# The inverse's first stage as pairs of 64-row tiles, w2 loaded in three pieces, and another total order of the work

## The chip, the cores and the metric

The kernel runs on one core of a Trainium2 chip. A core has five engines that run side by side and meet only at semaphores: PE (matrix multiply, with a separate path that loads weights, called PEld in the profile), ACT and DVE (elementwise work; these two can also read PSUM, the memory into which PE writes), POOL (elementwise work in SBUF) and SP, which here only issues DMAs. The metric is the device time of one launch in microseconds (us); smaller is better. Each kernel is run several times and the median counts. A profile is one execution recorded by the hardware.

## What is computed

Two sublayers follow each other: a gated long convolution over the normalised input, with a residual, and an MLP with the Mish activation over the normalised result, with a residual. 2048 positions (S), 640 channels (D), hidden width 1728, bf16 in and out.

```python
k_shift = sum(k_pad[:, t:t+S, :] * shift_k[:, ks-1-t] for t in range(4))   # 4-tap causal
kv  = k_shift * v
kv_f = rfft2(pad(kv, 2*S));  kf_f = rfft2(pad(ssm_k, 2*S))
y   = irfft2(kv_f * kf_f)[:S].astype(bf16)          # causal convolution, one per channel
A   = layernorm(q) * (y + kv * ssm_D)
h   = q + A
f   = einsum("bsd,df->bsf", layernorm(h), w1) + b1
act = f * tanh(softplus(f))                          # Mish
out = h + einsum("bsf,fd->bsd", act, w2)
```

## The kernel before

The transforms are matmuls with cosine and sine tables. Channels are held in five groups of 128 (dc 0 to 4); in one group four channels and 32 places make the 128 partitions. Positions are split as t = 16 t1 + t2, so that a transform over 4096 points becomes a 128-point one (stage 1), a small one with twiddles for each of 128 frequencies f (stage 2), and their inverses. The stages, with the names that the order below uses:

- **d_...**: loads. n is ssm_k (five pieces), k, v and x (the input q) four pieces each, g the 4 MB table of stage 2 (eight), sk the tiny shift_k, cst a table for stage 1 and masks, dr ssm_D, w1 and w2 the MLP's weights, t2m the table of the inverse's second stage. DMAs of SP go out in SP's order, and each waits until the DMA eight before it (over all queues) has landed. d_cst, d_sk and d_dr are issued by ACT.
- **k1pe, k1ev**: ssm_k transposed on PE, and copied out of PSUM. dadd adds ssm_D to its first point.
- **cfpe, coef, wsh**: shift_k spread over the partitions by one matmul; DVE copies it, POOL makes four banded matrices (wsh0 to 3) of it.
- **ktpe, ktev, ktsh**: k transposed; **kspe, kv**: the 4-tap filter as matmuls with wsh, and the product with v on DVE.
- **s1kpe, s1kev / s1vpe, s1vev**: stage 1 for ssm_k and for kv, 20 groups each. A group is 16 matmuls into one PSUM buffer of 1024 columns and one copy out of it ("eviction").
- **s2kpe, s2kev / s2vpe, s2vev**: stage 2, 22 groups for ssm_k, 20 for kv (8 for channel groups 0 and 1, 4 for group 2, 8 for 3 and 4). It overwrites its own input. All 22 for ssm_k are needed before the **sw** copies: ten DMAs inside SBUF that exchange real and imaginary rows.
- **pr**: 20 products of the two spectra on DVE, four for each channel group.
- **i1pe, i1ev**: the inverse's first stage (I1), 20 groups, four for each channel group; a group's matmuls need all four products of it.
- **i2a/i2b/i2pe, y**: the inverse's second stage, one step for each of the 16 row tiles of 128 positions, needing all I1 evictions; y is its eviction.
- **ln1, ln1p, lnx**: the input's layernorm (statistics on DVE, a power on POOL, the normalised tile by ACT or POOL). **wb, h, bn, pow, hc**: product, residual, statistics, power, normalised result; **tr** transposes it by DMA, the first two tiles on PE (**trpe, trev**).
- **m1pe, hb**: first MLP matmul in five units of 256, 256, 512, 512, 512 positions, Mish on ACT. **m2pe, res, d_out**: second matmul, residual, store. In m2pe the last 64 hidden rows of two row tiles are done as a pair of matmuls on 64 rows each (L671).

There is no scheduler at run time. ORDER (L26) lists 660 operations in one total order by name; the engines execute theirs in this order and wait by semaphores for what others must have done. A token `name@2` puts the result in PSUM buffer 2 (there are four, ps0 to ps3, of 1024 fp32 columns); `:d`, `:a`, `:p` choose DVE, ACT or POOL where there is a choice; evictions without a letter go to ACT, except k1ev and ktev, which go to DVE. `_ordered` (L108) reads it. The evictions run through `ev` (L259): L261 on ACT, L263 on DVE.

I1 multiplies the product tile (as weights, 128 rows of real and imaginary parts) with two tables, a12, 128 by 128 each. Each of these is zero except where the channel index of row and column agree, four channels in all:

```python
for dgl in range(8):
    b, l = dc * 8 + gi * 2 + dgl // 4, dgl % 4
    for k in range(2):
        nc.tensor.matmul(pz[:, dgl, :], KS[:, k, b, :, l], a12[:, k, :], start=k == 0, stop=k == 1)
```

SBUF areas are shared over time: the tile ks holds first the spectra (KS, two halves of 20480 columns), then the MLP's activations, w2 (from column 20480) and the convolution's row tiles tt (from column 30720).

Of the kernel before, what the change touches and what calls it, by code (L numbers as in the profile page):

```python
# [13 lines left out]
BF16 = mybir.dt.bfloat16  # L14
# [12 lines left out]
d_dr wz idn d_n0 cz wm@0 small lane d_n1 d_cst d_sk d_n2 warm d_n3 d_n4 d_g0 dsel dcol dadd0 d_k2 k1pe0@1 d_k3 dadd1:p k1pe1@2 d_a12 k1ev0b d_k0 k1ev0  # L27
s1kpe0_3@3 k1ev1 s1kpe0_1@0 s1kev0_3 d_k1 s1kpe0_0@1 dadd2 s1kev0_1 s1kpe1_3@2 s1kev0_0:d dadd3:p d_g4 s1kpe0_2@3 k1pe2@0 s1kev0_2 dadd4:p d_g1
s1kev1_3 kz b1pe@1 k1pe4@3 k1ev2 c_b1 cfpe@2 k1pe3@1 k1ev4:a coef d_v0 s1kpe2_0@0 k1ev3 wsh1 s1kpe2_1@2 s1kev2_0 s1kpe4_3@3 d_g7 s1kev2_1:d s1kpe3_1@1
s1kev4_3 s1kpe2_2@0 wsh3 s1kpe1_0@2 s1kev3_1 d_v1 s1kev2_2:d s1kpe4_1@3 d_g2 s1kev1_0 s1kpe3_2@1 s1kev4_1:d s1kpe1_2@0 s1kev3_2 d_g6 ktpe0_0@2 wsh2  # L30
ktpe0_3 ktpe0_2 s1kev1_2 ktpe2_0@3 ktpe2_3 ktpe2_2 d_v2 ktpe2_1 ktpe0_1 ktev2 ktpe1_0@1 ktev0:a ktpe1_1 ktpe1_3 ktpe1_2 s1kpe3_3@0 d_g5 ktev1 ktsh2
s1kpe4_0@3 s1kev3_3 s1kpe1_1@2 ktsh0 s1kev4_0:d d_v3 s1kpe4_2@1 wsh0 s1kev1_1 s1kpe3_0@0 s1kev4_2:d s1kpe2_3@3 s1kev3_0 d_g3 ktpe4_0@2 ktpe4_2 ktpe4_3
s1kev2_3 ktsh1 ktpe3_0@1 ktpe4_1 ktpe3_3 ktev4 ktpe3_1 ktpe3_2 s2kpe_6@0 s2kpe_12@3 ktev3 s2kev_6 kspe0_0@2 s2kev_12 s2kpe_18@0 kv0_0 ktsh3 kspe2_0@1
s2kev_18 ktsh4 s2kpe_42@3 kv2_0 kspe3_0@2 s2kev_42 s2kpe_96@0 kv3_0 s2kpe_24@1 s2kev_96 kspe4_0@3 s2kev_24 kspe1_0@2 kv4_0 s2kpe_108@0 kspe1_1@1 kv1_0
s2kev_108 s2kpe_72@3 kspe0_1@0 d_x1 s2kev_72 kv1_1 d_x0 s2kpe_66@2 s2kpe_102@3 s2kev_66 kv0_1 kspe4_1@1 s2kev_102 s2kpe_120@2 kv4_1 kspe3_1@0
s2kev_120 s2kpe_126@3 kv3_1 s2kpe_78@1 s2kev_126 s2kpe_0@2 s2kev_78 s2kpe_114@3 s2kev_0:d s2kpe_36@0 s2kev_114 s2kpe_54@1 s2kev_36:d s2kpe_84@2
s2kev_54 s2kpe_60@3 s2kev_84 ln1_0 kspe2_1@1 s2kev_60 s2kpe_48@0 kv2_1 ln1p0 s1vpe0_2@2 s2kev_48 s1vpe1_1@3 s1vev0_2:d s1vpe2_1@1 d_x2 s1vev1_1
s1vpe1_0@0 d_x3 s1vev2_1 s1vev1_0:d s1vpe4_3@2 s1vpe3_2@3 s1vev4_3 s1vpe0_0@1 s1vev3_2:d s1vpe2_2@0 s1vev0_0 s2kpe_90@2 s1vpe1_2@3 s1vev2_2 s2kev_90:d
# [8 lines left out]
pr4_32 i1pe1_0@0 i1ev2_0 i1pe2_2@3 pr4_64 i1ev1_0 i1pe2_1@2 ln1_8 i1ev3_2 i1pe2_3@0 i1ev2_2 ln1_6 ln1p8 i1pe4_3@1 i1ev2_3 ln1_11 i1pe4_0@3 ln1p6
i1ev2_1 i1ev4_3:d i1pe4_2@0 i1ev4_0 lnx6:p i1pe4_1@2 ln1_4 i1ev4_2 ln1p11 i2a1@1 d_w2a i1ev4_1 ln1_14 i2a0@3 d_w2b ln1p4 d_w2c i2b1 ln1_10 i2a2@0 y1
i2b0 i2pe4@2 y0 wb1 i2pe5@1 y4 h1 i2pe8@3 wb0 y5 h0 i2b2 i2a3@2 y8 bn1 i2pe15@1 y2 i2b3 i2pe12@3 bn0 y15 pow1 i2pe13@0 y3 i2pe11@1 pow0 y12 hc1 wb2
trpe1@2 y11 i2pe7@3 hc0 y13 h2 trpe0@1 trev1:a wb3 i2pe6@0 bn2 trev0:a i2pe10@2 y7 m1pe0_3@1 h3 lnx11 pow2 bn3 m1pe0_2@3 y6 hc2 y10 pow3 ln1_7  # L50
# [16 lines left out]
SW_PIECES = 1  # L67
V_PIECES = 4
# [57 lines left out]
def _make_tables():  # L126
# [3 lines left out]
    g = np.arange(16, dtype=np.float64)  # L130
    T = {}
# [13 lines left out]
    T["g"] = np.moveaxis(G, 4, 6).reshape(128, 128 * 128)  # L145
# [14 lines left out]
    a12 = np.stack([np.moveaxis(A1, 0, 2).reshape(128, 128), np.moveaxis(A2, 0, 2).reshape(128, 128)], axis=1)  # L160
# [3 lines left out]
    T["t2m"] = np.concatenate([t2m.reshape(128, 4096), a12.reshape(128, 256)], axis=1)  # L164
# [5 lines left out]
def kernel(  # L170
# [49 lines left out]
    a12_t = cpool.tile([P, 256], BF16, name="a12_t")  # L220
# [24 lines left out]
    w2 = ks[:, 20480:20480 + 15 * D].rearrange("p (c d) -> p c d", c=15)  # L245
    tt_s = [ks[:, 30720 + t * D:30720 + (t + 1) * D] for t in range(NT)]
# [219 lines left out]
    d_a12 = load("d_a12", a12_t[:], dram["t2m"][:, 4096:4352])  # L466
# [3 lines left out]
    for dc in range(NDC):  # L470
        for gi in range(4):
            p_ = pt()

            def pe(e, gi=gi, p_=p_, dc=dc):
                pz = p_.f32().rearrange("p (g n) -> p g n", g=8)
                for dgl in range(8):
                    b, l = dc * 8 + gi * 2 + dgl // 4, dgl % 4
                    for k in range(2):
                        nc.tensor.matmul(pz[:, dgl, :], KS[:, k, b, :, l], a12[:, k, :], start=k == 0, stop=k == 1)  # L479
# [10 lines left out]
    def emit_w2(e):  # L490
        nc.sync.dma_start(w2[:, 0:13, :], B_w2[0:13 * P, :].rearrange("(c p) d -> p c d", p=P))
    d_w2 = [OP("d_w2a", "sp", i1_pes, emit=emit_w2)]
# [241 lines left out]
```

## Time and profile before

| | |
|---|---|
| median of 3 runs | 225.41 us |
| lowest, highest | 225.4, 225.89 us |
| profiled execution, first to last instruction (span) | 223.5 us |
| PE busy in it | 214.0 us, 96% |
| DVE, ACT busy | 133.2 and 133.0 us, 60% and 59% |
| POOL busy | 58.9 us |
| moved by DMA | 30.98 MB, mean 139 GB/s |

The profile gives the execution's time as its span; what lies around the span (the launch and the last store's end) is in the runs' times, which are 1.9 us longer at the median.

How to read its rows. A row of a timeline is: start, length (both us), engine, line, operation, out<-in by tile name, shapes, count; in brackets the idle time of that engine before it and what ended it. A row of the groups is: line, engine, operation, shape, count | busy us, mean ns of one | idle us before them. A DMA row ends with KB each and us from issue to landing. Matmuls overlap in the pipeline, so the length of one is more than its share; busy time divided by the count is nearer to what one costs. A row of the chain is start, length, engine, tile and line.

### The profile page before, as it was taken

The page shows a single profiled execution, that of the slowest core. Times are in us where ns is not written, and L with a number is a line of the kernel's source. Part 1 is how long each engine was busy: PE and PEld are TensorE (multiplying, and loading weights), DVE is VectorE, ACT ScalarE, POOL GpSimd, SP SyncE. Part 2 cuts the span into 40 slices and gives each one's busy share as a digit, 9 for nine tenths or more (in the row PEclk, how much of TensorE's full clock was granted, in tenths as well). Part 3 has the DMA queues.
Part 4 walks back from the last instruction along what each step waited for, and adds up shares of the span by engine and source line. Part 5 has one row for each costly group of instructions (what it writes and reads, how often), then busy time and mean ns, then how long its engine had stood idle before and what let it go on. Part 6 is the DMA issues. An engine that isn't in the chain of part 4 may idle for free.

```text
span 223.5 us, 6119 instructions
## 1 busy us (share of the span) xinstructions
PE 214.0 (96%) x2645; PEld 157.6 (70%) x2650; DVE 133.2 (60%) x232; ACT 133.0 (59%) x182; POOL 58.9 (26%) x120
## 2 busy tenths in 40 slices
PE   7899999999879999889999999999999999999994
PEld 2899999888869999458877644444567444766763
DVE  2776899999989999889878999100002200022122
ACT  2389888999999999999983015565600075200000
POOL 5147620102860005347887523100000000000000
PEclk9999999999999999999999999999999999999999
DMA  5999994372991789303004443500001100010211
GB/s 181 390 413 409 412 374 121 143 239 93 375 415 69 258 331 290 124 0 62 1 0 62 84 123 91 118 0 0 3 0 59 59 3 0 0 56 6 76 54 49
DMA packets 19563, 30.98 MB, mean 139 GB/s; under 512 B 10704, under 2 KB 14928, under 8 KB 18768
## 3 DMA queue, kind: packets, MB, share of 16 engines
q1 hardware_dynamic: 19104, 30.46, 39.0%
q8 instruction: 21, 0.34, 0.7%
q10 hardware_dynamic: 336, 0.12, 0.2%
q14 instruction: 6, 0.05, 0.1%
q0 software_dynamic: 96, 0.00, 0.0%
HBM read 20.42 MB, written 2.62 MB: 103 GB/s over the span
## 4 chain that ended last, share of the span: by engine, by line
PE 70%; DVE 13%; DMA 9%; ACT 4%; issue 2%; SPq 1%; POOL 1%; DVEq 0%
PE ps L663 26%; PE ps L598 25%; DVE ks L461 6%; DMA ks<-in_B_w_dram 4%; DMA ks<-ks 3%; PE ps L396 3%; PE ps L422 3%; ACT uv L261 3%; DMA ks<-in_A_ssm_k_dram 3%; PE ps L341 2%; PE ps L376 2%; DVE ks L263 2%; PE ps L357 2%; DVE ra L362 1%; PE ps L397 1%
## 5 line engine op out<-in xcount | busy, mean ns | idle before, releaser
L620 ACT ACTIVATE ks<-ps,b1s 128x512 bf16<-128x512 f32 (+1 forms) x69 | 36.1, 610 | 42.8 <-PE ps L598 30.3
L663 PE MATMUL ps<-ks 128*128 128x320 bf16 (+2 forms) x420 | 58.4, 299 | 0.0
L598 PE MATMUL ps<-G 128*128 128x512 bf16 (+1 forms) x320 | 57.0, 336 | 0.3
L688 DVE TENSOR_TENSOR rb<-ps,rb 128x640 bf16<-128x640 f32 x15 | 11.7, 816 | 68.9 <-PE ps L671 66.5
L663 PEld LDWEIGHTS <-ks 128*128 128x128 bf16 x420 | 40.6, 98 | 17.2 <-issue 1.3
L598 PEld LDWEIGHTS <-G 128*128 128x128 bf16 x325 | 31.3, 98 | 24.4 <-issue 1.1
L261 ACT CAST uv<-ps 128x1024 bf16<-128x1024 f32 x49 | 45.2, 1197 | 0.0
L261 ACT CAST ks<-ps 128x960 bf16<-128x960 f32 (+3 forms) x49 | 39.8, 905 | 8.1 <-PE ps L397 5.0
L461 DVE TENSOR_TENSOR ks<-ks,uv 128x2048 bf16<-128x2048 bf16 x20 | 23.1, 1225 | 0.7 <-DMA ks<-ks 0.7
L422 PEld LDWEIGHTS <-G 128*128 128x128 bf16 x512 | 20.9, 96 | 3.1 <-issue 2.5
L479 PE MATMUL ps<-a_t,ks 128*128 128x128 bf16 x320 | 18.8, 219 | 0.4 <-DVE ks L461 0.3
L479 PEld LDWEIGHTS <-ks 128*128 128x128 bf16 x320 | 18.3, 113 | 0.7 <-DVE ks L461 0.6
L422 PE MATMUL ps<-uv,G 128*128 128x64 bf16 (+1 forms) x384 | 12.8, 186 | 1.8 <-ACT uv L261 1.8
L544 DVE BATCH_NORM_STATS2 st<-rb 128x6 f32<-128x320 bf16 x32 | 14.0, 478 | 0.1
L515 POOL TENSOR_SCALAR ve<-mv 128x1 f32<-128x1 f32 x16 | 4.7, 292 | 34.9 <-DVE mv L511 34.2
L510 DVE BATCH_NORM_STATS2 st<-rb 128x6 f32<-128x320 bf16 x32 | 13.7, 471 | 0.0
L263 DVE CAST uv<-ps 128x1024 bf16<-128x1024 f32 x11 | 12.9, 1204 | 0.1
L362 DVE TENSOR_TENSOR ra<-ps,rb 128x1024 bf16<-128x1024 f32 x10 | 11.9, 1222 | 0.7 <-PE ps L358 0.5
L524 POOL TENSOR_SCALAR ra<-rb,r,nmr 128x640 bf16<-128x640 bf16 x8 | 8.9, 1118 | 10.0 <-PE ps L397 9.3
L422 PE MATMUL ps<-ks,G 128*128 128x160 bf16 x128 | 11.2, 230 | 0.0
L396 PE MATMUL ps<-cst,ra 128*64 128x128 bf16 x160 | 10.6, 219 | 0.7 <-ACT uv L261 0.5
L263 DVE CAST ks<-ps 128x1024 bf16<-128x1024 f32 (+1 forms) x9 | 10.5, 1197 | 0.5 <-PE ps L422 0.3
(71 smaller groups left out, 256.1 us busy)
## 6 DMA issues: line engine op xcount, KB each, us to landing
ks<-ks SPq DMA_DIRECT2D x10, 512.0 KB, 6.2
G<-tab_g SPq DMA_DIRECT2D x8, 512.0 KB, 11.4
ks<-in_A_ssm_k_dram SPq DMA_DIRECT2D x5, 512.0 KB, 6.4
ra<-in_A_k_dram SPq DMA_DIRECT2D x4, 640.0 KB, 10.9
rb<-in_A_v_dram SPq DMA_DIRECT2D x4, 640.0 KB, 11.5
rb<-in_A_q_dram SPq DMA_DIRECT2D x4, 640.0 KB, 5.1
out_dram<-rb SPq DMA_DIRECT2D x15, 160.0 KB, 1.9
G<-in_B_w_dram SPq DMA_DIRECT2D x5, 432.0 KB, 6.0
```

Of the source, the lines that this page charges most:

```text
L261: nc.scalar.copy(o, i)
L263: nc.vector.tensor_copy(o, i)
L362: nc.vector.tensor_tensor(kv_w[:, m, :, 8 * h:8 * h + 8, :], p_.f32().rearrange("p (l t d) -> p d t l", l=4, t=8), raw_v[:, 8 * h:8 * h + ...
L396: nc.tensor.matmul(ps[0:64, dgl, :], lhs, mc, start=True, stop=True)
L422: nc.tensor.matmul(p_.f32()[:, o:o + n], g_v[:, f, :], src[:, :, f, :], start=True, stop=True)
L461: nc.vector.tensor_tensor(o, o, v, ALU.mult)
L479: nc.tensor.matmul(pz[:, dgl, :], KS[:, k, b, :, l], a12[:, k, :], start=k == 0, stop=k == 1)
L510: nc.vector.bn_stats(st1[:, t, hh, :], xt(t)[:, hh * 320:(hh + 1) * 320])
L544: nc.vector.bn_stats(st2[:, t, hh, :], xt(t)[:, hh * 320:(hh + 1) * 320])
L598: nc.tensor.matmul(ph[:, o:o + w], w1[:, dc, fc * P:fc * P + P], lt[:, dc, 0:w], start=dc == 0, stop=dc == NDC - 1)
L620: nc.scalar.activation(hb[:, fc, 0:n], p_.f32()[:, i * 512:i * 512 + n], ACT.Mish, bias=b1s[:, fc:fc + 1], scale=1.0)
L663: nc.tensor.matmul(p_.f32()[:, o:o + n], lhs, w2[:, k, cols:cols + n], start=fc == 0, stop=single and fc == 13)
```

## The change

Three things change.

**I1.** The four channels that shared 128 partitions in I1 are split into two pairs: the g table's columns are ordered so that the first 64 rows hold two channels and the last 64 rows the other two. The a12 tables shrink to 64 by 64 (held twice, once for each half of the partitions). Where a group was 16 matmuls of 128 rows by 128 columns, it is now 32 of 64 rows by 64 columns: for each former one, one on rows 0 to 63, which writes the first half of the PSUM buffer, and one on rows 64 to 127, which writes the second half. The eviction moves the same 1024 columns, read as runs of two from the two halves in turn. PE has 2970 matmuls instead of 2650.

**w2.** The big load of 13 row blocks becomes three of 5, 4 and 4 (d_w2a0, d_w2a1, d_w2a2); the areas of w2 and tt inside ks change places, so that w2 lies over channel groups 2 to 4 of the second half. SP issues 78 DMAs instead of 76.

**The order.** All of ORDER is new. What it alters, counted from the two lists:

| | before | after |
|---|---|---|
| shift_k's load (d_sk) | ACT's third instruction | ACT, behind the second eviction |
| PE up to cfpe | k1pe0 to 2, k1pe4, b1pe, five s1k groups | k1pe0 to 2, five s1k groups |
| behind cfpe, ahead of stage 2 | k1pe3, 15 s1k groups, ktpe | k1pe3, k1pe4, 15 s1k groups, ktpe |
| s2k groups done on PE before the s1v stage proper | 20 (two come among s1v) | 22, with two s1v groups among them |
| s1k, s1v evictions on DVE | 6, 9 | 4, 6 |
| s2v evictions on DVE | 1 | 5 |
| I1 evictions on DVE | 1 (i1ev4_3) | 2 (i1ev4_2, i1ev4_3) |
| k1ev, ktev on ACT | one each | none |
| y on DVE; trev0 | none; ACT | y0, y11; DVE |
| input statistics (ln1) on DVE ahead of the first wb | 10 | 6 |
| lnx on POOL | 8 | 10 |
| first swap copies (sw) | after two late s2k groups | right behind the last s2k group |
| d_w2... | all ahead of y | w2c, w2a0, w2a1 behind I1; w2b and w2a2 behind the transposes of tiles 2 and 3 |
| b1's load and transpose (small, b1pe) | at the start | in the s1v stage, in stage 2 |

The diff, cut:

```diff
@@ ORDER, the beginning and the places named above
-d_dr wz idn d_n0 cz wm@0 small lane d_n1 d_cst d_sk d_n2 warm d_n3 d_n4 d_g0 dsel dcol dadd0 d_k2 k1pe0@1 d_k3 dadd1:p k1pe1@2 d_a12 k1ev0b d_k0 k1ev0
-s1kpe0_3@3 k1ev1 s1kpe0_1@0 s1kev0_3 d_k1 s1kpe0_0@1 dadd2 s1kev0_1 s1kpe1_3@2 s1kev0_0:d dadd3:p d_g4 s1kpe0_2@3 k1pe2@0 s1kev0_2 dadd4:p d_g1
...
+idn d_dr d_n0 wz warm d_n1 lane d_n2 d_cst dsel dcol dadd0:p wm@0 dadd1 k1pe0@1 k1ev0b d_n3 k1pe1@2 dadd2:p d_n4 d_g0 s1kpe0_3@3 d_k2 k1ev0 dadd4:p
+s1kpe0_2@0 k1ev1 d_k3 s1kev0_3 k1pe2@1 s1kpe0_1@2 s1kev0_2 d_a12 d_sk cz s1kev0_1 s1kpe1_0@3 dadd3 s1kpe0_0@0 s1kev1_0 k1ev2 cfpe@1 k1pe3@2 k1pe4@3
...
+i1pe4_1@1 i1pe4_3@2 i1ev2_3 i1ev4_3:d i1pe4_0@0 i1ev4_1 i2a0@3 i2a1@1 i1ev4_0 i2b1 y1 i2b0 i2pe5@2 ln1p6 y0:d wb1 wb0 i2pe10@0 ln1p3 y5 lnx3:p i2a3@1
...
+W2_PARTS = ((0, 5), (5, 9), (9, 13))
...
-    T["g"] = np.moveaxis(G, 4, 6).reshape(128, 128 * 128)
+    T["g"] = G.reshape(2, 16, 4, 128, 2, 16, 2, 2).transpose(0, 1, 2, 3, 6, 5, 7, 4).reshape(128, 128 * 128)
...
-    A1 = np.zeros((2, 16, 4, 2, 16, 4))
-    A2 = np.zeros((2, 16, 4, 2, 16, 4))
-    for dl in range(4):
+    A1 = np.zeros((2, 16, 2, 2, 16, 2))
+    A2 = np.zeros((2, 16, 2, 2, 16, 2))
+    for dl in range(2):
...
-    w2 = ks[:, 20480:20480 + 15 * D].rearrange("p (c d) -> p c d", c=15)
-    tt_s = [ks[:, 30720 + t * D:30720 + (t + 1) * D] for t in range(NT)]
+    w2 = ks[:, 30720:30720 + 15 * D].rearrange("p (c d) -> p c d", c=15)
+    tt_s = [ks[:, 20480 + t * D:20480 + (t + 1) * D] for t in range(NT)]
...
-                pz = p_.f32().rearrange("p (g n) -> p g n", g=8)
+                pz = p_.f32().rearrange("p (h g n) -> p h g n", h=2, g=8)
                 for dgl in range(8):
                     b, l = dc * 8 + gi * 2 + dgl // 4, dgl % 4
                     for k in range(2):
-                        nc.tensor.matmul(pz[:, dgl, :], KS[:, k, b, :, l], a12[:, k, :], start=k == 0, stop=k == 1)
+                        for h in range(2):
+                            r = slice(64 * h, 64 * h + 64)
+                            nc.tensor.matmul(pz[:, h, dgl, :], KS[r, k, b, :, l], a12[r, k, :], start=k == 0, stop=k == 1)
...
-                ev(e, Z[:, dc, :, gi * 32:gi * 32 + 32].rearrange("p j (g l) -> p j g l", l=4), p_.f32().rearrange("p (g j l) -> p j g l", g=8, l=4))
+                ev(e, Z[:, dc, :, gi * 32:gi * 32 + 32].rearrange("p j (g h l) -> p j g h l", h=2, l=2), p_.f32().rearrange("p (h g j l) -> p j g h l", h=2, g=8, l=2))
...
-        nc.sync.dma_start(w2[:, 0:13, :], B_w2[0:13 * P, :].rearrange("(c p) d -> p c d", p=P))
-    d_w2 = [OP("d_w2a", "sp", i1_pes, emit=emit_w2)]
+    d_w2 = [load(f"d_w2a{i}", w2[:, c0:c1, :], B_w2[c0 * P:c1 * P, :].rearrange("(c p) d -> p c d", p=P), deps=i1_pes) for i, (c0, c1) in enumerate(W2_PARTS)]
```

More of the change, by code (lines that the diff above doesn't have):

```diff
@@ L31 @@
[L31 to L38, printed above, removed]
@@ L47 @@
[L47 to L50, printed above, removed]
@@ new lines @@
+s2kev_90 s1vpe0_3@2 s2kpe_30@3 kv2_1 s2kev_120 kspe4_1@0 s2kpe_96@1 s1vev0_3 s2kpe_54@2 s2kev_30 s2kpe_48@3 s2kev_96 s2kev_48 ln1_1 s1vpe0_0@1 kv4_1
+s1vpe0_2@0 s2kev_54:d s1vev0_2:d sw3_0 s1vpe0_1@3 s1vev0_0 sw0_0 small s1vpe3_2@2 s1vpe1_3@1 s1vev0_1 s1vev3_2:d s1vpe2_3@0 s1vpe1_1@3 s1vpe1_2@2
+s1vev1_3 s1vev2_3 ln1_2 s1vpe3_3@1 s1vev1_1 sw1_1 s1vev1_2:d s1vpe4_1@0 sw4_0 s1vev4_1 s1vpe4_2@3 ln1p0 s1vev3_3:d s1vev4_2 s1vpe2_2@2 s1vev2_2:d
+s1vpe3_1@0 s1vpe2_1@1 sw2_0 s1vpe4_3@3 s1vev2_1:d s1vev3_1 s2v0pe_112@2 ln1p2 sw0_1 s2v0pe_48@0 s1vev4_3 s1vpe4_0@1 s2v0pe_32@3 s2v0ev_112 ln1_4
@@ new lines @@
+h1 y10 h0 i2pe13@3 y13 bn1 i2b3 i2pe4@2 y3 i2pe6@0 i2a2@3 bn0 i2b2 wb3 y6 i2pe11@1 d_w2c pow1 y2 i2pe7@0 pow0 hc1 wb2 i2pe8@3 lnx6:p y4 y7 y8 hc0
+trpe1@2 i2pe12@0 h3 trpe0@3 trev0 bn3 h2 bn2 pow3 pow2 trev1:a hc3 ln1_8 i2pe15@2 hc2 d_w2a0 y11:d ln1p8 y12 m1pe0_3@3 m1pe0_0@0 y15 ln1_5 hb0_3
+m1pe0_1@2 hb0_0 wb6 m1pe0_4@3 ln1p5 m1pe0_2@0 ln1_10 ln1_12 d_w2a1 ln1p10 ln1_7 wb4 tr3 hb0_1 h6 h4 tr2 d_w2b hb0_4 hb0_2 bn4 bn6 m1pe0_5@2 ln1p7
+m1pe0_6@1 w2z hb0_5 m1pe1_0@3 m1pe1_4@0 hb0_6 lnx8:p ln1_13 hb1_0 ln1_11 hb1_4 m1pe1_1@2 ln1_15 lnx5 m1pe1_5@1 hb1_1 m1pe1_3@3 ln1p12 lnx7 d_w2a2 pow4
@@ L219 @@
     nmr2 = cpool.tile([P, NT], F32, name="nmr2")
-    a12_t = cpool.tile([P, 256], BF16, name="a12_t")
+    a12_t = cpool.tile([P, 128], BF16, name="a12_t")
     b1b = cpool.tile([14, P], BF16, name="b1b")
@@ L465 @@
     i1_pes, i1_evs = [], []
-    d_a12 = load("d_a12", a12_t[:], dram["t2m"][:, 4096:4352])
+    d_a12 = load("d_a12", a12_t[:], dram["t2m"][:, 4096:4224])
     s1v_in = lambda c0, c1: [s1["v", dc, gi][0] for dc in range(NDC) for gi in range(4) if dc * S + gi * 512 < c1 and dc * S + gi * 512 + 512 > c0]
```

48 lines of the change are left out of this document (25 added, 23 removed).

## The prediction, made before the changed kernel ran

> **What bounds the kernel now.** I read the page's slices first, then busy time by stretch, then single rows. The slices say which engine is full when:
>
> ```profile
> span 223.5 us, 6119 instructions
> ...
> PE   7899999999879999889999999999999999999994
> DVE  2776899999989999889878999100002200022122
> ACT  2389888999999999999983015565600075200000
> PEclk9999999999999999999999999999999999999999
> ```
>
> PE looks full everywhere, but from slice 8 to slice 17 ACT shows nines too, and DVE nearly so; from slice 18 on PE alone is full. The clock never drops. Cut at the places where that changes (us; then busy us and count for PE, PEld, DVE, ACT, POOL; clock; DMA share; GB/s):
>
> ```profile
> 9.00:27.30 18.30, 18.07 (x393) 17.02 (x388) 13.93 (x17) 16.82 (x17) 10.65 (x14) 1.00 1.02 412
> 27.30:44.00 16.70, 16.60 (x279) 16.15 (x278) 15.99 (x17) 14.32 (x17) 1.27 (x3) 1.00 0.63 230
> 44.00:91.20 47.20, 43.62 (x1043) 40.66 (x1041) 45.83 (x59) 47.15 (x52) 14.78 (x28) 1.00 0.70 259
> 91.20:99.40 8.20, 7.62 (x61) 4.41 (x61) 7.07 (x19) 7.89 (x14) 2.63 (x6) 1.00 0.03 6
> 99.40:220.30 120.90, 120.64 (x819) 75.21 (x822) 46.81 (x114) 45.30 (x82) 26.15 (x57) 1.00 0.16 40
> ```
>
> Three regimes. To 44 us PE is the tightest, with the loads at 412 GB/s beside it. From 44 to 91.2 the two engines that empty PSUM are: ACT is idle 0.05 of 47.2 us. From 99.4 PE works 120.64 of 120.90 us without a wait worth naming. So the end is the first MLP matmul plus 121 us, and the question is by how much that matmul moves. It hangs on the last eviction of the inverse's first stage (I1):
>
> ```profile
> 55.23 35.92 ACT L261 CAST uv<-ps 128x1024 bf16<-128x1024 f32 x39
> 91.51 6.66 ACT L261 CAST ks<-ps 128x640 bf16<-128x640 f32 x11 [0.36 <-DMA ks<-in_B_w_dram]
> 50.05 3.48 DVE L263 CAST uv<-ps 128x1024 bf16<-128x1024 f32 x3
> 53.44 0.88 DVE L510 BATCH_NORM_STATS2 st<-rb 128x6 f32<-128x320 bf16 x2
> 54.48 2.30 DVE L263 CAST uv<-ps 128x1024 bf16<-128x1024 f32 x2
> 65.28 19.39 DVE L461 TENSOR_TENSOR ks<-ks,uv 128x2048 bf16<-128x2048 bf16 x17 [0.69 <-DMA ks<-ks]
> 92.31 0.49 DVE L538 TENSOR_TENSOR ks<-ks,ra 128x640 bf16<-128x640 bf16 x1 [0.49 <-ACT ks L261]
> 97.94 1.43 ACT L261 COPY G<-ps 128x640 bf16<-128x640 bf16 x2
> 99.49 1.25 PE L598 MATMUL ps<-G 128*128 128x256 bf16 x10
> ```
>
> ACT's 39 evictions end at 91.15 at 0.92 us each; on DVE a product takes 1.14 (19.39/17), a cast 1.13 (three from 50.05 to 53.44), an input-statistics step 1.04 (53.44 to 54.48). The wait at 91.51 is put down to a w2 load that lands later, so it was the PE's, for the last I1 group. From 91.15 a chain (y, two products, statistics, POOL's power, normalise, transpose, copy) takes 8.3 us to the MLP.
>
> **The pairs.** A 128-row group was 16 matmuls of 128 columns; it is now 32 of 64 rows and 64 columns, two side by side.
>
> ```profile
> L479 PE MATMUL ps<-a_t,ks 128*128 128x128 bf16 x320 | 18.8, 219 | 0.4 <-DVE ks L461 0.3
> L422 PE MATMUL ps<-uv,G 128*128 128x64 bf16 x256 | 9.0, 191 | 1.5 <-ACT uv L261 1.5
> 125.72 0.57 PE L663 MATMUL ps<-ks 128*128 128x320 bf16 x3
> 126.23 0.45 PE L671 MATMUL ps<-ks 64*128 64x320 bf16 x4
> 126.61 0.58 PE L663 MATMUL ps<-ks 128*128 128x320 bf16 x3
> 115.70 10.60 PE ps L663 x78
> ```
>
> Now a group costs 18.8/20 = 0.94 us. A 64-column matmul takes 9.0/256 = 0.035. If pairs overlap, 16 x 0.035 = 0.56; if they take turns, 1.12. The only 64-row pairs in the trace are L671's: four 320-column matmuls from 126.23 to 126.61, 0.38 us, where four one after the other at 10.60/78 = 0.136 would need 0.54. They overlap, with some 0.1 for going in and out of that tiling. I take 0.56, and 0.1 for each of eight such switches between stages: PE falls from 18.8 to 12.0 us, 7 us less. On the path that is worth next to nothing: the groups are emptied at 0.92 us each by ACT, so PE at 0.94 only just kept pace and a faster PE waits for PSUM. Up to 0.92 a group nothing is lost either. The eviction reads the same 1024 columns in runs of two rather than four; the nearest row,
>
> ```profile
> L261 ACT CAST ks<-ps 128x960 bf16<-128x960 f32 x18 | 16.3, 973 | 2.7 <-PE ps L422 2.5
> ```
>
> breaks its read into short runs over both halves of the buffer too and costs 16.3/18 = 0.91 for 960. Per element that is 0.94 ns against 0.90: between 0 and 0.04 x 18 = 0.7 us; I take 0.
>
> **w2 in three pieces** adds two issues on SP, which is idle then. The last piece stands behind the transposes of row tiles 2 and 3, so it is issued near 103 and is needed when m2 begins, near the 115.70 above:
>
> ```profile
> ks<-in_B_w_dram SPq DMA_DIRECT2D x1, 2080.0 KB, 8.7
> ```
>
> Even at the whole load's 8.7 us it lands by 112; I take 0, and without that cover a late piece would hold m2 itself. The exchange of the w2 and tt areas asks nothing new: y waits for all I1 groups either way.
>
> **The order, front part.** It moves shift_k's load (d_sk) on ACT's queue from ahead of all evictions to behind the second one, and PE's coefficient matmul (cfpe) needs it. Behind cfpe in PE's queue stand k1pe3, k1pe4 and 15 of the 20 k groups; ACT and DVE live on these.
>
> ```profile
> dful<-in_A_ssm_D_dram ACTq DMA_DIRECT2D x1, 5.0 KB, 2.2
> cst<-tab_cst ACTq DMA_DIRECT2D x1, 104.0 KB, 4.3
> sk_r<-in_A_shift_k_dram ACTq DMA_DIRECT2D x1, 5.0 KB, 4.9
> 9.01 3.76 ACT L261 CAST ks<-ps 128x1024 bf16<-128x1024 f32 x4 [5.00 <-PE ps L397]
> 12.18 1.22 PE L376 MATMUL ps<-ident,ks 128*128 128x128 bf16 x16
> 12.25 1.23 DVE L263 COPY ks<-ps 128x2048 bf16<-128x2048 bf16 x1 [1.12 <-PE ps L498]
> 27.45 0.93 PE L422 MATMUL ps<-ks,G 128*128 128x160 bf16 x11
> ```
>
> ACT's first eviction starts near 9.0 in both (0.94 each), so PE reaches cfpe after the fifth k group, near 11.8. The load is issued between 9.4 (second eviction started) and 10.9 (ended), and lands 2.2 (quiet queue) to 4.9 us later (loads running, cst ahead): 11.6 to 15.8. I take 9.4 + 4.3 = 13.7, cst's row, since sk now has no big load ahead of it on its queue but full loads beside it. Then two transposes (2 x 1.22), one k group (0.5) to 16.7; ACT's eleven remaining k evictions at 0.92 to 26.8; one DVE copy (1.2) that PE stands behind: 28.0. The s2k stage starts at 28.2 instead of 27.45. Through it PE is the bound: before it spent the 16.7 us above; the new list has two s2k groups, two s1v groups and four switches more (2 x 0.42 + 2 x 0.45 + 0.4 = 2.1), so it ends at 47.0 and its last evictions near 48.1. At that point both orders have emptied 24 groups of s2k and s1v: the old one had reached the same count at 48.1. The lag is paid for by work moved in.
>
> **The order, eviction part.** ACT before: 47 evictions from 48.0 to 91.15 (0.917 each). After: 45 and the small bias copy, 45 x 0.917 + 0.2 = 41.5, to 89.6. DVE after: 11 evictions and 20 products at 1.14, two statistics at 1.04: 37.4, to 85.6; waits 0.5 (the old list had 0.69 for a swap load at 65.28 alone; the swaps now start some 5 us sooner, before the products need them): 86.1; then two more statistics and the two evictions of I1's last channel group that DVE now does, 4.4: 90.5, 0.65 sooner than 91.15. That the list does only four statistics there instead of nine is what pays.
>
> **The transition and the MLP.** The chain stays as it was, with one copy (trev0) moved from ACT, where it lasted to the MLP's start, to DVE: the row at 97.94 gives 0.77 for the second copy; on DVE between 0.4 (640 of the 2048 in 1.23) and 0.77; I take 0.4, 0.35 gained. In the MLP the same matmuls run. The five postponed statistics stand ahead of row tiles 4 to 7, but later rows' products move behind these: I count 9 + 9 + 9 + 8 + 10 steps before the last of their normalisations against 13 + 11 + 11 + 9 + 6, 32.7 us against 32.5 at these rows' prices. PE had room there:
>
> ```profile
> 126.20 0.80 DVE L559 TENSOR_SCALAR rw<-rb,mv,r 128x640 bf16<-128x640 bf16 x2
> 130.69 0.32 PE ps L598
> ```
>
> Normalised by 127.0, plus a transpose of 2.6, against 130.69: about 1 us left. So 0.
>
> **Sum.** -0.65 - 0.35 = -1.0 on a span of 223.5: 222.5. The median of the runs, 225.41, is 1.9 above the span; with that, **224.4**.
>
> **Rivals.**
> (a) shift_k lands before PE asks for it (11.6): everything from cfpe on is 2.0 us sooner, 222.4. For it: the small first load took 2.2. Against: both loads under traffic took 4.3 and more.
> [...]
> (b) Slower: the issue waits for the second eviction's end and takes sk's own 4.9: landing at 15.8, PE, then ACT and DVE empty-handed 2.1 us longer, 226.5. It decides from a landing at 14.7 on, where the gain is gone. For it: 412 GB/s of loads then; against: its old delay had 104 KB ahead of it.
> (c) Pairs whose weight loads do not hide.
>
> ```profile
> L479 PEld LDWEIGHTS <-ks 128*128 128x128 bf16 x320 | 18.3, 113 | 0.7 <-DVE ks L461 0.6
> L671 PEld LDWEIGHTS <-ks 64*128 64x128 bf16 x28 | 0.8, 94 | 1.8 <-issue 1.8
> ```
>
> A 64-row load lasts 94 ns, hardly less; 32 in turn at 18.3/320 = 0.057 make 1.8 us a group, 17 us more of PE in I1: 242 or so. L671's loads did overlap, so this is unlikely.
> [...]
> (d) The postponed statistics make m1 of row tiles 4 to 7 wait: one room of 1 us against POOL's heavier list; if its two added normalisations (1.1 us each, by the group of eight below) come ahead, 1.5 us more, 225.9.
>
> ```profile
> L524 POOL TENSOR_SCALAR ra<-rb,r,nmr 128x640 bf16<-128x640 bf16 x8 | 8.9, 1118 | 10.0 <-PE ps L397 9.3
> ```
>
> **How the numbers follow.** Forecast 0.44 (own range 223.7 to 225.1: waits of 0 to 1.2, eviction pattern 0 to 0.7), (a) 0.20, (b) 0.24, (c) 0.04, (d) 0.08. Range 222.2 to 226.9: from (a) to (b), a little beyond each, with only (c) and tails left out. 0.3% is 0.68 us, about what can be told from no change. Faster: (a) and 0.72 of the forecast, 0.52. Same: the rest of it and half of (d), 0.16. Slower: (b), (c) and half of (d), 0.32.
>
> **What would show it.** Right: PE idle before the coefficient matmul of 1 to 3 us, released by shift_k's load; first s2k matmul near 28.2; swaps issued near 48; ACT unbroken to about 89.6; a pair group in 0.5 to 0.7 us with PE waiting for ACT between groups; first MLP matmul near 98.4, then 121 us without gaps. Wrong: an ACT gap inside I1, an I1 eviction over 0.95, a gap before the third unit's m1, or the MLP stretch longer than 121.

## The result, and the profile after

The changed kernel takes 235.56 us, the median of four runs (235.07 to 237.07), against 225.41 for the kernel before: a ratio of 1.046, 95% interval 1.0425 to 1.0495. It is 10.1 us slower where 1 us of gain was forecast. One run of one kernel below (the changed kernel with shift_k early and x3 behind x2) took 231.66 us, 1.6% above that kernel's fastest of 228.04, and is left out of its median. The profiled execution took 235.38 us. Its slices:

```profile
span 233.6 us, 6767 instructions
...
PE   7949999999858854898999999999999999999994
...
DVE  1728689899999997489999969910062000002241
ACT  2436779999996992987788021651400654400000
...
PEclk9988999999997965999999999999999999999999
```

Two things are new. Counted from 0, PE has holes at slice 2 and from slice 10 to 16, and the granted clock, which was full throughout before, falls in the same places or right behind them. In ACT the unbroken stretch of nines has a 6 and a 2 in it. By stretch (columns as in the prediction; the first row is PE's wait for shift_k; then cut at the first s2k matmul, the end of the s2k stage, the last I1 eviction and just ahead of the first MLP matmul):

```profile
11.40:15.20 3.80, 0.35 (x14) 0.19 (x9) 0.14 (x1) 2.33 (x3) 0.31 (x6) 1.00 1.03 405
15.20:31.65 16.45, 16.36 (x312) 15.39 (x313) 12.37 (x14) 10.37 (x11) 9.37 (x6) 0.90 1.02 411
31.65:50.30 18.65, 18.57 (x323) 17.97 (x321) 17.06 (x20) 17.07 (x20) 4.75 (x11) 1.00 0.32 108
50.30:100.50 50.20, 38.53 (x1320) 35.33 (x1318) 44.64 (x47) 43.12 (x48) 10.76 (x17) 0.86 0.54 200
...
109.00:230.10 121.10, 120.99 (x823) 75.19 (x822) 52.06 (x129) 42.44 (x78) 29.05 (x64) 1.00 0.20 46
```

The MLP took its 121 us as forecast: from its first matmul to PE's last, both profiles have 121.06 us. The loss lies ahead of it. Where it arose is told by the last I1 evictions on ACT and the first MLP matmul, from the timelines of the two engines:

```profile
96.63 3.88 ACT L262 CAST uv<-ps 128x1024 bf16<-128x1024 f32 x4
...
109.32 1.91 PE L599 MATMUL ps<-G 128*128 128x256 bf16 x16
```

I1 ends at 100.51 instead of 91.15 (+9.36); the transition takes 8.81 instead of 99.49 - 91.15 = 8.34 (+0.47); the rest of the span is +0.3. What PE waited for, from its list of waits (total us, times, longest):

```profile
PE ps L482 <- issue: 6.4, 3, 4.0
PE ps L305 <- DMA sk_r<-in_A_shift_k_dram: 3.4, 1, 3.4
PE ps L423 <- issue: 3.1, 2, 2.7
```

So there is the late shift_k (L305), and a releaser that the kernel before did not have in this list: "issue", that is, PE waits for nothing that the profile shows. The chain of waits (where "issue" can be any engine's) says that this lay on the path. First from 60 to 101 us of the changed kernel, then from 44 to 92 us of the kernel before:

```profile
by line: ACT uv L262 38.7%; issue 27.9%; PE ps L482 12.4%; PE ps L423 8.0%; DVE st L511 3.9%; DVE uv L264 3.0%; POOL r L517 2.8%; PE ps L397 1.3%; POOL ve L516 1.1%; POOL nmr L518 0.6%; DVE mv L512 0.5%; ACT b1s L500 0.4%; PE ps L398 0.1%; 
```

```profile
by line: DVE ks L461 28.7%; DMA ks<-in_B_w_dram 17.0%; DMA ks<-ks 13.9%; ACT uv L261 12.0%; issue 6.1%; PE ps L396 5.2%; PE ps L479 4.2%; PE ps L422 3.4%; DVE uv L263 2.6%; ACT ks L261 2.3%; PE ps L397 2.2%; DVE ra L362 2.0%; SPq L450 1.1%;
```

**What "issue" is.** Among the DMA queues the pages list two for instructions. The larger has these rows, in the changed kernel and in the kernel before (packets, MB, share):

```profile
q8 instruction: 23, 0.38, 0.7%
```

```profile
q8 instruction: 21, 0.34, 0.7%
```

0.38 MB in 23 packets is 16 KB each, and PE executes 2970 matmuls, as many weight loads and some semaphore instructions, 5961 records in all: 23 packets of 256 make 5888. In the records of the trace each packet can be laid beside PE's own instructions, numbered from 0. The table is worked out from these two kinds of records of the changed kernel; the gap is from start to start, so it holds what PE's last instruction before it took:

```
block entered | its successor's packet    | successor: PE's last before, its first, gap
 no.    at us | starts at us   landed at  |  no.       us       us       us
1985    58.14 |   60.96           61.89   | 2241     62.62    63.24    0.62
2241    63.24 |   68.24           69.28   | 2497     67.73    70.60    2.87
2497    70.60 |   71.72           72.99   | 2753     74.28    74.33    0.05
2753    74.33 |   75.98           77.02   | 3009     78.57    78.59    0.03
3009    78.59 |   81.25           82.20   | 3265     81.58    83.50    1.92
3265    83.50 |   88.38           89.33   | 3521     86.54    90.79    4.25
3521    90.79 |   92.01           92.93   | 3777     94.16    94.51    0.35
3777    94.51 |   95.61           96.78   | 4033     97.22    98.07    0.85
```

Every gap of PE over 0.1 us in the table lies at instruction 193 + 256k, and behind each PE goes on 1.3 to 1.6 us after a packet has landed, whatever operation stands there. So in this trace PE gets its instructions in blocks of 256. In the table the next block's packet starts 1.1 to 5.0 us after PE has entered the block before it, and where PE is through that block earlier than 1.3 to 1.6 us after the packet's landing, it stands, for up to 4.25 us from start to start. In the kernel before, with 21 packets, none of these boundaries between 48 and 89 us shows a gap over 0.06 us: there PE spent 4.4 to 7.5 us on a block.

Behind three of PE's idle stretches (the wait for shift_k among them) the clock is halved. Windows cut where the granted clock changes:

```profile
12.42:15.83 3.41, 0.65 (x9) 0.60 (x10) 0.39 (x2) 1.31 (x2) 0.00 (x0) 1.00 1.02 401
15.83:19.24 3.41, 3.41 (x42) 3.23 (x42) 2.27 (x5) 0.00 (x0) 2.72 (x2) 0.50 1.03 418
67.03:70.44 3.41, 0.81 (x26) 0.73 (x26) 3.41 (x4) 2.77 (x4) 2.34 (x1) 1.00 0.59 214
70.44:73.86 3.42, 3.26 (x113) 3.26 (x113) 3.42 (x4) 1.99 (x3) 0.00 (x0) 0.50 0.03 7
80.69:84.10 3.41, 1.40 (x69) 1.30 (x67) 3.41 (x4) 3.41 (x5) 0.00 (x0) 1.00 0.96 307
84.10:94.34 10.24, 6.23 (x231) 5.96 (x225) 8.17 (x10) 5.73 (x7) 0.00 (x0) 0.50 0.62 248
```

Here a stretch of 3.41 us in which PE worked 0.65, 0.81 or 1.40 us is followed by one, or three, of 3.41 at 0.50.

### The profile page after: what moved, and what is told of

It reads as the page before. It is cut to its first block, busy times and chain, and to the rows that moved or that the text cites. A ratio compares the mean times of both kernels' runs of the same rounds, so it can differ in the third digit from the quotient of the medians.

```text
span 233.6 us, 6767 instructions
## 1 busy us (share of the span) xinstructions
PE 212.4 (91%) x2970; PEld 155.2 (66%) x2970; DVE 139.3 (60%) x237; ACT 126.7 (54%) x175; POOL 61.5 (26%) x122
## 4 chain that ended last, share of the span: by engine, by line
PE 70%; DVE 8%; ACT 8%; issue 7%; DMA 5%; POOL 1%; SPq 0%; ACTq 0%; DVEq 0%
PE ps L664 25%; PE ps L599 24%; ACT uv L262 7%; PE ps L423 5%; PE ps L397 3%; DVE uv L264 3%; DMA sk_r<-in_A_shift_k_dram 3%; DMA ks<-in_A_ssm_k_dram 2%; PE ps L342 2%; PE ps L482 2%; PE ps L377 2%; PE ps L358 2%; DVE st L511 1%; PE ps L359 1%; PE ps L606 1%
## 5 line engine op out<-in xcount | busy, mean ns | idle before, releaser
L599 PE MATMUL ps<-G 128*128 128x512 bf16 (+1 forms) x325 | 57.8, 337 | 0.1
L664 PEld LDWEIGHTS <-ks 128*128 128x128 bf16 x420 | 40.6, 98 | 17.7 <-issue 1.3
L262 ACT CAST ks<-ps 128x960 bf16<-128x960 f32 (+3 forms) x49 | 40.6, 900 | 16.4 <-PE ps L398 13.2
L262 ACT CAST uv<-ps 128x1024 bf16<-128x1024 f32 x47 | 44.1, 1047 | 7.2 <-PE ps L482 4.5
L462 DVE TENSOR_TENSOR ks<-ks,uv 128x2048 bf16<-128x2048 bf16 x20 | 24.1, 1272 | 0.0
L482 PE MATMUL ps<-a_t,ks 64*128 64x64 bf16 x640 | 14.9, 209 | 7.3 <-issue 6.4
L482 PEld LDWEIGHTS <-ks 64*128 64x128 bf16 x640 | 14.1, 118 | 8.2 <-issue 7.8
L264 DVE CAST uv<-ps 128x1024 bf16<-128x1024 f32 x13 | 15.3, 1212 | 5.2 <-ACT uv L262 4.5
L516 POOL TENSOR_SCALAR ve<-mv 128x1 f32<-128x1 f32 x16 | 3.9, 245 | 52.7 <-DVE mv L512 52.3
L525 POOL TENSOR_SCALAR ra<-rb,r,nmr 128x640 bf16<-128x640 bf16 x10 | 12.6, 1267 | 0.9 <-POOL nmr L518 0.7
L550 POOL TENSOR_SCALAR ve<-mv 128x1 f32<-128x1 f32 x16 | 4.4, 275 | 32.1 <-DVE mv L546 31.4
## 6 DMA issues: line engine op xcount, KB each, us to landing
G<-tab_g SPq DMA_DIRECT2D x8, 512.0 KB, 10.3
```

The costliest lines, as they stand in the source:

```text
L262: nc.scalar.copy(o, i)
L264: nc.vector.tensor_copy(o, i)
L462: nc.vector.tensor_tensor(o, o, v, ALU.mult)
L482: nc.tensor.matmul(pz[:, h, dgl, :], KS[r, k, b, :, l], a12[r, k, :], start=k == 0, stop=k == 1)
L525: nc.gpsimd.tensor_scalar(lnx_s[t % 9], xt(t), r1[:, t:t + 1], nmr1[:, t:t + 1], ALU.mult, ALU.add)
L599: nc.tensor.matmul(ph[:, o:o + w], w1[:, dc, fc * P:fc * P + P], lt[:, dc, 0:w], start=dc == 0, stop=dc == NDC - 1)
```

## The experiments

All ratios are against the kernel before, run beside each kernel. Theory F below is: two separate losses, the late shift_k and PE's starved instruction fetches.

**shift_k early.** The changed kernel, one token of its order moved:

```diff
 d_cst
+d_sk
 dsel
...
 d_a12
-d_sk
 cz
```

> The changed kernel with shift_k's load alone moved: to ACT's queue right behind cst's, where the kernel before had it. Theory F (two losses: late shift_k in front, starved instruction fetches of PE in the inverse): in the changed kernel PE stood 3.6 us before the coefficient matmul, then ran 3.4 us at half clock, and its first s2k matmul came at 31.65 us of the trace instead of 27.45. That whole loss goes: first s2k matmul at 27.2 to 27.6, no half clock before 60 us, time 235.6 - 4.2 = 231.4 (231 to 232). The stalls in the inverse stay. Rival O (the end is set in the inverse by loads and swaps that do not start earlier, so the front loss is swallowed there): 233.5 or more.

230.62 us (1.020, 1.0137 to 1.0263): 4.9 less than the changed kernel. PE's timeline has the first s2k matmul where it was before:

```profile
26.96 0.58 PE L423 MATMUL ps<-ks,G 128*128 128x160 bf16 x6
```

The clock is full to 65 us, and 4.9 us is gone, a little more than F's 4.2 (its range began at 231); the stalls in the inverse stayed (up to 3.7 us at instruction 2497). The front loss is carried in full to the end, as F said.

**128-row groups, with and without the early shift_k.** The changed kernel with I1's matmuls (and the tables that go with them) as before:

```diff
-for h in range(2):
-    r = slice(64 * h, 64 * h + 64)
-    nc.tensor.matmul(pz[:, h, dgl, :], KS[r, k, b, :, l], a12[r, k, :], start=k == 0, stop=k == 1)
+nc.tensor.matmul(pz[:, dgl, :], KS[:, k, b, :, l], a12[:, k, :], start=k == 0, stop=k == 1)
```

> The changed kernel, its order and its w2 pieces kept, with I1 back as groups of sixteen 128-row matmuls (tables g and a12 as before). Theory F: the 640 PE instructions (320 matmuls and 320 weight loads) that go were what made PE overtake its instruction fetches; no PE stall over 1 us between 60 and 100 us, granted clock 1.0 there, last I1 eviction some 5 us sooner, time near 230.5 (229.5 to 231.5). Rival O (the new order itself starves the evictions, the pairs are harmless or help): 234.5 to 237, and the ACT gaps in the inverse stay.

> Both edits together: what is left is the new order and the w2 pieces with 128-row groups and an early shift_k. Theory F: both losses are separate and add up, 235.6 - 4.2 - 5 = 226.4 (225 to 227.5), granted clock 1.0 throughout. If the new order in itself gains the 1 us that was forecast for it, with the rest of the forecast right, 224.4 or a little less. Rival O: above 231.

233.25 us (1.0308, 1.0242 to 1.0375) and 229.09 us (1.0133, 1.0077 to 1.0189). F missed both by some 2.7 us, rival O too. PE's waits and ACT's last evictions of the first of the two:

```profile
PE ps L423 <- issue: 2.9, 2, 2.7
```

```profile
84.01 12.94 ACT L262 CAST uv<-ps 128x1024 bf16<-128x1024 f32 x14
97.19 1.01 ACT L262 CAST uv<-ps 128x1024 bf16<-128x1024 f32 x1 [0.24 <-PE ps L480]
```

In I1 the stalls are gone, as F said, and ACT runs without a hole. But the stall at instruction 2497 stays, since up to there the two kernels issue the same instructions: it belongs to the new order, not to the pairs. F had put all the stalls on the pairs. And the 128-row groups cost the PE time that the pairs save: from 44 to 101 us PE's I1 matmuls are the largest item of this kernel's chain of waits, 27.8%. So trading one for the other in this order is worth only 1.5 to 2.3 us (with shift_k early the runs of the two kernels overlap by half a us).

**Pairs alone.** The kernel before with the reverse of that edit.

> The kernel before with I1 alone as 64-row pairs (and the tables g and a12 that go with them); order, shift_k and w2 as before. Theory F: the stalls of PE at its instruction fetches come here too, two or more of over 1.5 us between 64 and 92 us, each ended about 1.4 us after an instruction packet has landed, with half clock behind them: 228 to 231. Rival O (the order is at fault): 225.4 within 0.7, no such stall. Forecast's rival (c) (weight loads of pairs do not hide, 1.8 us a group everywhere): above 238.

231.20 us (1.0219, 1.0157 to 1.0281), just above F's range. PE's waits, and ACT's evictions:

```profile
PE ps L481 <- issue: 8.3, 3, 4.5
```

```profile
83.69 1.01 ACT L261 CAST uv<-ps 128x1024 bf16<-128x1024 f32 x1 [1.50 <-PE ps L481]
85.40 5.59 ACT L261 CAST uv<-ps 128x1024 bf16<-128x1024 f32 x6 [0.69 <-PE ps L481]
94.77 2.84 ACT L261 CAST uv<-ps 128x1024 bf16<-128x1024 f32 x3 [3.78 <-PE ps L481]
```

The gaps are at instructions 3521 (3.4 us) and 4033 (4.7 us): the same numbers modulo 256, in another order and at other groups. Their packets started 4.6 us after PE had entered the block, under the loads of w1, t2m and w2; the one between them, at 3777, started 1.05 us after, and its gap was 0.8.

**Pairs, with w1 out of the way.** The same kernel, w1's five loads moved on SP's queue, and the two small w2 loads with them ahead of the big one:

```diff
-d_w14
-d_w10
-d_w11
-d_w12
-d_w13
 d_t2m
...
+d_w2b
+d_w2c
+d_w14
+d_w10
+d_w11
+d_w12
+d_w13
 d_w2a
...
-d_w2b
-d_w2c
```

> The kernel before with I1 as pairs (231.2 us), and the five loads of w1 moved on SP's queue behind the two small w2 loads, which wait for I1's last group; only t2m is left to load during I1. Theory F (the pairs' stalls are instruction packets that come late under loads: 4.6 us after entering the block, against 1.1 to 1.3 us where nothing is loaded): the stalls of 3.4 and 4.7 us at PE's 3521st and 4033rd instruction shrink to 0.3 to 1.4 us each, half clock mostly gone, last I1 eviction 4 to 6 us sooner; 225.5 to 228, if w1 is not itself late for the first MLP matmul. Rival C (PE's clock halves because a pair fills the array by half, and that is what slows I1): half clock stays, 229.5 or more.

225.53 us (1.001, 0.999 to 1.003): all 5.8 us are back, with the pairs in place. The profiled execution took 226.58 us, 1.0 above the median. PE's timeline in I1:

```profile
78.18 2.99 PE L481 MATMUL ps<-a_t,ks 64*128 64x64 bf16 x128 [0.63 <-issue]
81.64 2.37 PE L481 MATMUL ps<-a_t,ks 64*128 64x64 bf16 x102 [0.47 <-issue]
```

The stall still comes at every block (the first of these rows has just 128 matmuls, with as many loads), but it is 0.4 to 0.9 us, and ACT, by its timeline, does not notice:

```profile
84.00 8.41 ACT L261 CAST uv<-ps 128x1024 bf16<-128x1024 f32 x9
```

The one long stall (2.3 us, before 74.6) has a packet that was wanted at 68.4 while t2m, now right behind the swaps, was being moved, and started at 72.4; the clock is halved only behind it, from 76.2 to 79.6. Rival C is out: from there on the pairs ran at full clock.

**x3 among the swaps.** In the new order x3's load (640 KB) stands among the ten swap loads. Put there in the kernel before:

```diff
-d_x3
...
 sw4_1
+d_x3
```

> The kernel before with one load moved on SP's queue: x3 (640 KB) from behind s1v's beginning, near 45.5 us, to the middle of the ten swap loads (behind sw4_1), where the new order has it. No PE instruction is added. Theory F (PE starves when an instruction packet comes late, and x3 among the swaps is what made packet 8 come 5 us after its block was entered instead of 2.2 to 2.6): the packet that is asked for near 57.7 or 63.2 starts 4 us or more later, PE stands 1.5 to 3 us at the 2497th or 2753rd of its instructions, 3.4 us of half clock may follow; 227.5 to 229.5. Rival P (the new order's stall comes from its own place of the swaps or from PE's denser work there, not from x3): 225.4 within 0.7, no stall.

And taken out, with shift_k early, in the new order with 128-row groups and with pairs:

```diff
-d_x3
...
 d_x2
+d_x3
```

> The changed kernel with 128-row groups and an early shift_k (229.1 us), and x3's load moved behind x2's, out of the swaps. Theory F: the stall of 3.4 us at PE's 2497th instruction shrinks to under 1 us, no half clock, 229.1 - 2.5 to 4.5, so 224.6 to 226.6. Rival P: the stall stays above 2.5 us, 228.5 to 229.5.

> The changed kernel with its pairs, shift_k early (230.6 us as such) and x3 moved behind x2. Theory F: the stall at the 2497th instruction goes as above, but x3 now adds to the loads under which the pairs fetch; 226.5 to 229. The difference to the same with 128-row groups is what pairs cost here. Rival P: 230 to 231.

225.57 us (0.9996, 0.9976 to 1.0016); 227.26 (1.0088, 1.0058 to 1.0118); 229.01 (1.0196, 1.0136 to 1.0256). F missed the first, and the second lies between its range and P's; the third is at the upper end of F's. With x3 among the swaps the kernel before has no stall, and its packets start 2.3 and 2.9 us after their blocks are entered, hardly later than the 2.6 and 2.2 without. The other two gain 1.8 and 1.6 us: the packet that had started 5.4 (128 rows) and 5.7 us (pairs) after its block was entered now starts 1.5 and 3.4 us after. So the place of x3 matters in the new order and not in the old one. Two things separate them. First, PE takes 4.5 us for a block in the new order's s2v stage, 5.5 and 6.6 us in the old one's blocks under the swaps. Under swaps a packet took, in the middle, some 2.7 us to start, 0.9 to land and 1.4 until PE ran, 5.0 in all: that makes short stalls in the new order and none in the old. Second, single packets of the new order start some 5 us or more after their block is entered, and that makes the long stalls. Why these packets and not others is not shown. The last two kernels are some 1.7 us apart, which is what the pairs cost here.

**x2 and x3 ahead of the swaps; w2 alone.** With shift_k early, 128-row groups in the first kernel, pairs in the second, which moves w1 too (the tokens' old places are not shown):

```diff
+d_x2
+d_x3
 sw3_0
...
 d_w2c
+d_w10
+d_w11
+d_w12
+d_w13
+d_w14
```

The third is the kernel before with the w2 part of the change (the areas of w2 and tt exchanged, three pieces):

```diff
-d_w2a
+d_w2a0
+d_w2a1
+d_w2a2
```

> The changed kernel with 128-row groups, shift_k early, and x2 and x3 loaded ahead of the first swap load, as in the kernel before. Theory F: what is left of stalls is the mean one: in the new order PE goes through a block of 256 instructions of s2v in 4.5 us, while under swaps a packet needs some 2.7 us to start, 0.9 to land and 1.4 until PE runs, 5.0; so 0.5 us each at two or three blocks, 1 to 2 us in all, no half clock: 225.8 to 227.3. If stalls of over 2.5 us stay with x3 gone from the swaps, x3 is not what made them.

> The changed kernel, pairs and order and w2 pieces kept, with its loads put where they do not meet the dense stretches of PE instructions: shift_k early, x2 and x3 ahead of the swaps, w1's five loads behind the first small w2 load. Theory F: the front loss, the long stall in s2v and the long stalls of I1 all go; left are some 0.4 to 0.9 us at a block, under ACT's evictions in I1: 225 to 226.8, 0.963 of clock becomes 0.99 or 1. If the forecast's order terms were right beneath the stalls, 224.4 to 225. Rival C (pairs at half clock are what is slow): above 228.

> The kernel before with the w2 part of the change alone: the w2 and tt areas exchanged, w2's thirteen blocks loaded in three pieces, one behind the other where the one load stood. Theory F and the forecast's term agree: nothing, 225.4 within 0.7. Rival W (two more issues on SP ahead of the transposes, or pieces that land later than the one load did): 226 or more, with the matmuls of m2 or the transposes of row tiles 2 and 3 waiting.

230.02 us (1.018, 1.0143 to 1.0216), 229.42 (1.0151, 1.0115 to 1.0187) and 225.45 (0.9998, 0.9982 to 1.0014). The first two are misses of F's: with both loads ahead, the swaps stand behind a longer queue (they land up to 10.3 us after they are issued instead of some 6.5), and five of six packets under them start 3.6 to 5.1 us after their blocks are entered; the long stall moves forward to instruction 1985 (2.9 and 2.6 us), and in the second kernel 2.0 and 2.3 us follow at the next two blocks. So it is not x3 by itself: the packets came later under the fuller queue. In the second kernel the stalls of I1, with w1 gone, are 0.4 to 0.6 us, as with the pairs in the old order. Its time lies where rival C was put, but its half clock, from 68.8 to 75.6, stands behind the stalls of s2v, and from 75.6 on the pairs have full clock. The w2 pieces, where the one load stood, are worth nothing either way.

**The change with its loads apart.** Pairs, order and w2 pieces kept; shift_k early, and these moved on SP's queue:

```diff
-d_x3
...
-d_w10
-d_w13
...
-d_w11
-d_w14
-d_x2
...
 d_w2c
+d_w10
+d_w11
+d_w13
+d_w14
+d_x2
+d_x3
```

> The changed kernel, pairs, order of the engines and w2 pieces kept; shift_k early, and four of w1's five loads, x2 and x3 behind the first small w2 load, so that only one w1 load and t2m are moved during I1 and only swaps during s2v. Theory F: as with x3 behind x2 (229.2 us, last I1 eviction at 93.6, stalls of 0.5 and 1.2 us under the swaps and of 2.7 and 2.3 in I1), but the stalls in I1 shrink to one of 1 to 2 us and the rest to 0.4 to 0.9: last I1 eviction at 91 to 92.5, 225.3 to 227.5, granted clock 0.99 or more. If it comes to 225.4 the new order is worth what the old one is, without its stalls; below 224.8 the forecast's order terms were right beneath them. Rival C or P: 229 or more.

226.53 us (1.0057, 1.0033 to 1.0080), within F's range: 9.0 of the 10.1 us are recovered by moving seven loads (shift_k's among them). It does not beat the kernel before. The profiled execution took 228.22 us, 1.7 above the median. PE in I1:

```profile
78.24 2.52 PE L482 MATMUL ps<-a_t,ks 64*128 64x64 bf16 x128 [1.16 <-issue]
81.97 2.58 PE L482 MATMUL ps<-a_t,ks 64*128 64x64 bf16 x128 [1.21 <-issue]
85.93 2.48 PE L482 MATMUL ps<-a_t,ks 64*128 64x64 bf16 x127 [1.38 <-issue]
89.65 0.53 PE L482 MATMUL ps<-a_t,ks 64*128 64x64 bf16 x21 [1.24 <-issue]
```

This is the plainest view of it: 128 matmuls in 2.5 us, then 1.2 us of nothing, with a period of 3.7 to 4.0 us though only one w1 load (432 KB) and t2m (1024 KB) are moved during I1. Four groups in 3.7 us are 0.93 a group, where the matmuls alone would allow 0.62.

In this profile I1 ends 0.9 us later than in the kernel before, and the transition is 0.5 longer. A third item, 1.1 us, lies in the MLP: PE waits for the transposes of the second unit.

```profile
109.25 3.00 PE L599 MATMUL ps<-G 128*128 128x256 bf16 x26 [1.07 <-DMA G<-rw]
```

The four kernels of the new order with 128-row groups have the same wait, of 0.5 to 1.4 us; the kernel before and the changed kernel have none. No experiment took it apart.

## Why the prediction was wrong, by its steps

The accounts close: 235.56 to 230.62 is shift_k (4.9); to 229.01 x3 (1.6); to 226.53 the loads of w1 and x taken out of I1 (2.5); and 1.1 is left to the kernel before.

**The bound and the MLP.** "First MLP matmul plus 121 us" held (121.06). "The clock never drops" was read off the kernel before and carried to one in which PE stands idle for 3 us at a time; that reading was not the change's to keep.

**The pairs: the step that failed.** The size was nearly right (128 pair matmuls in 2.5 us are 0.62 a group against 0.56), the loads overlap (640 of them, 118 ns long at the mean, were busy 14.1 us in all), rival (c) is out. What failed is "up to 0.92 a group nothing is lost". The step priced a group by how long its matmuls last and not by how many instructions it is. Sixteen matmuls became 32, with their loads 64 instructions; a block of 256 is four groups, and from one starved block of I1 to the next it took 3.4 to 4.0 us with little moving (in the changed kernel 3.56 us at a DMA share of 0.02) and 4.9 to 7.3 us under loads (there 4.91 at 0.83, and 7.29 at 0.93 with the clock at 0.54), 0.85 to 1.0 and 1.2 to 1.8 a group. The first is at the edge of the 0.92, the second far over it. The row of the instruction queue, with its 21 packets, stood on the page before. In the old order this alone cost 5.8 us.

**The front: the effect was rival (b)'s, its condition and its size were not.** shift_k's issue and its path to PE, from ACT's timeline and from the rows of the tile:

```profile
9.19 0.35 ACTq L271 DMA_DIRECT2D sk_r<-in_A_shift_k_dram  x1
...
10.88 2.84 ACT L262 CAST ks<-ps 128x1024 bf16<-128x1024 f32 x3 [0.23 <-PE ps L398]
19.56 1.01 ACT L262 CAST ks<-ps 128x1024 bf16<-128x1024 f32 x1 [5.83 <-PE ps L398]
```

```profile
DMA to landing us min/median/max: 6.0/6.0/6.0
```

It was issued earlier than the 9.4 assumed and took 6.0 us, more than either row that bounded it (2.2 and 4.9): the argument that a shorter queue ahead would shorten it was wrong. Its first packet began only at 12.7, 3.5 us after the issue. What held it there is not shown. It landed at 15.1 (13.7 forecast, 15.8 in (b)), 1.4 us after the forecast, which at (b)'s own rate would have put the first s2k matmul at 29.6. It came at 31.8: PE waited 3.4 us, then ran 3.4 us at half clock (some 1.7 us lost, a term that no rival had), and ACT was idle 5.8 us. The sentence "the lag is paid for by work moved in" did not hold either: the loss came through to the end in full.

**The evictions and the order.** ACT to 89.6 and DVE to 90.5 did not come about in any profile of the new order: with 128-row groups and x3 moved away, the last I1 eviction ended at 91.9, with the loads apart at 92.1, against 91.15 (the second of these executions was 1.7 us over its kernel's median, so what its median run had is not known). The price of an eviction was right: in the old order, with w1 out of the way,

```profile
L261 ACT CAST uv<-ps 128x1024 bf16<-128x1024 f32 x49 | 45.4, 1098 | 1.2 <-PE ps L481 0.7 <-PE ps L422 0.5
```

45.4/49 = 0.93, against 45.2/49 = 0.92 in the kernel before, so runs of two cost nothing that matters. What the step left out is that the new order has PE issue s2v's small matmuls in a row under the swaps, a block in 4.5 us against a fetch of 5.0 in the middle and of 8 at the worst. In this it was the same omission as for the pairs.

**The transition** was forecast 0.35 shorter and came out 0.5 longer; in the other kernels of the new order it took 8.3 to 8.8 us, and no experiment took it apart. **The w2 pieces** at 0 were right, shown alone (0.9998). **Rival (d)** did not occur: the MLP shows no gap at its third unit. The wait that the new order can have stands one unit sooner, at the second.

**What stays open.** The packets of all fourteen profiles between 40 and 112 us, laid beside the DMA records, show when one is late. Where the DMA engines were under a tenth busy from the block's entry to the packet's start (70 packets), it started 1.8 us after the entry at the latest. Where they were over 85% busy (67 packets), it took 0.9 to 5.7 us, 2.7 in the middle. So in these profiles a packet was late only with loads in flight, and the runs that moved loads agree. How late, the share does not tell: in one kernel a packet under the swaps waited 3.6 us and the next 1.5. Loads in smaller pieces were not tried.

## What to carry to other kernels

Count PE's instructions as well as its time: matmuls and weight loads together, in blocks of 256, against some 3.7 us a block with the DMA queues nearly empty and 5 to 8 us under full ones, as these runs have it. By these figures splitting matmuls into more, smaller ones is worth what it saves only where PE stays above that, and a load that nobody waits for can be the one that holds PE up (with the pairs in the old order, moving w1's loads gave back 5.7 us). A load of 5 KB on an otherwise short queue took 6 us while another queue ran at 400 GB/s; what a chain of engines hangs on goes out first.

## What was not expected of the hardware

- "Issue" as a releaser of PE meant a late instruction packet in each case that could be laid beside the packets: gaps of 0.3 to 4.7 us, ended 1.2 to 1.6 us after a packet had landed.
- One idle stretch of 2 to 4 us cost a second time: half clock for 3.4 us, and for 10.2 us where one stall followed another. Windows tell it better than stalls. Cut into windows of 3.41 us as the clock's records set them, all fourteen profiles have, up to PE's last matmul, 15 windows at full clock in which PE was busy for 1.83 us or less, and each is followed by half clock; behind those with 1.97 us or more there is none; of the two in between, one is. So a stall of 2.6 us that fell across two windows (x2 and x3 ahead of the swaps, with pairs) cost no half clock.
